# A copy of X opens Y's bank: fewer VectorE adds, and other orders, in a spectral layer with a gated feed-forward block

## The chip, the cores and the metric

The kernel runs on one core of one Trainium2 chip. A core has five engines, each with its own queue of instructions that it works off strictly in order: TensorE (PE; its weight loads are shown apart as PEld), VectorE (DVE), ScalarE (ACT), GpSimd (POOL) and SyncE (SP), which here only issues DMAs. They meet through semaphores. PE writes its products to PSUM, eight banks of 128 partitions by 512 fp32 numbers; DVE and ACT read and write PSUM, POOL works in SBUF alone here. The metric is the device time of one execution in microseconds (us), the median of several runs.

## What is computed

```python
# x: 2048 x 448; F1, F2: complex DFT matrices over sequence and features
def A(x):                       # FNet mixing: Real(DFT_seq(DFT_hidden(x)))
    a = x @ dft_hid_re.T
    b = x @ dft_hid_im.T
    return dft_seq_re @ a - dft_seq_im @ b
def B(x):                       # GEGLU
    return (gelu(x @ w_gate) * (x @ w_up)) @ w_down      # 448 -> 1792 -> 448
h  = x + A(layernorm(x))
out = h + B(layernorm(h))
```

Everything comes in and goes out as fp32.

## The kernel before

Every fp32 operand is split into two fp16 parts, a high one written by ACT (`hi_part`, L100) and the remainder, written by DVE (`lo_part`, L104 and L106). A product is then three products of parts, all summed in one PSUM bank. The matrix products that can be are done with seven products of half blocks instead of eight, after a scheme of Strassen's kind, so sums of blocks are formed ahead of the splits, and the results are put together from several banks.

There are four stages. **The feature DFT** (F) handles sixteen tiles of 128 rows of x. For each, `x_stats` takes mean and variance (DVE), `root` the square root (ACT), `rstd` the reciprocal with a correction step (DVE), `x_norm` the normalized row and its high part, `x_lo` the remainder. `x_turn_pe` transposes the first four tiles on PE and copies the result to SBUF with ACT (L371); the others are transposed by DMA (`x_turn`). `feature_mm` makes 22 products of 448 columns into two banks (L408), `feature_out` splits them into the operands `b` of the next stage; of three units (`S_UNITS`) it only copies them to fp32, POOL forms sums (`feature_sums`), and `feature_split` splits those.

**The sequence DFT** (U) has eight passes, each over eight units of the DFT matrices `wr`. `seq_sums` forms sums for a unit of S_UNITS (DVE), `seq_split` makes the fp16 parts `ws` (three buffers), `seq_mm` multiplies (L494): 24 products of 448 columns for a plain unit, 42 of 224 columns for an S unit, into four banks X, Y, Z, W. Two sets of four banks serve alternating passes. `seq_out` puts the four banks together with x, which `h_tile` has loaded, to two rows of h. Passes 0 to 3 are followed at once by the second layernorm's work (`ffn_moments`, `ffn_rstd`, `ffn_norm_act`, `ffn_sums`, `ffn_split`, `ffn_transpose`). The weights of gate and up are prepared in the same stretch (class `Weights`) and stored to `w_dram`.

The order in both DFT stages is set by a table. `slots` lists the F and U entries in PE's order; `plan(n, rank, what)` hangs other work on slot n, and the loop at the end records what hangs on a slot by rank and then the slot's products. Since engines work in order, that order is each engine's queue. The first three slots are written out by hand ahead of the loop.

**Gate/up** runs over 56 steps t (four quarters q of 512 rows, fourteen slices f of 128 hidden columns). A step makes seven products (class `GateUp`, L872): X takes A11·B11 and later A12·B21, Y takes S2·T2, then S3·T3, then A22·T4, and Z takes S1·T1 and S4·B22, six or five matmuls of 256 columns each and 39 in all. X alone (`u1`, L910, an ACT copy) is needed three times: `plus` (L882, DVE) adds it to Y as it stands after each of Y's three products. ACT makes the gelu of X (`g1`, L923) and of `c12` (L946); POOL makes the two multiplications (L939, L948). `gw_load(t + 2)` (L952, SP) loads the weights of step t + 2 into the buffer that step t - 1 used; there are three. In the first quarter ACT, DVE and POOL also prepare the down weights (`down_hi`, `down_lo`, `down_sums`).

**Down** is interleaved with steps 14 to 55 (L815, 21 products of 224 columns in each step), from sums that POOL and DVE form (`dn_sums`) and splits (`dn_split`); the last quarter is multiplied at the end (L1035).

## Time and profile before

| | |
|---|---|
| median of 3 runs | 738.9 us (736.61, 738.9, 739.53) |
| the profiled execution | 736.13 us, of which the span of its instructions is 734.3 us |
| PE busy | 712.6 us of the span, 5800 matmuls |
| DVE busy | 577.6 us |
| ACT busy | 322.0 us |
| POOL busy | 265.7 us |
| first product of a feature tile | 9.42 us from the start of the span |
| sequence DFT and its preparation | until 370.07 us |
| gate/up and down | 370.07 to about 698 us |

Times in the views are counted from the start of the span. "Idle before" a row is the time in which its engine stood still just ahead of it, with the instruction that ended the wait. A matmul's duration in the rows covers its way through the array; matmuls overlap, so one of 256 columns lasts 0.273 us but the next starts after about 0.11.

### The profile page before, as it was taken

To read this page: it belongs to the slowest core of one execution; us is meant where nothing else is said; L and a number is where in the kernel's file an instruction comes from. 1 tells how busy PE (TensorE), PEld (TensorE's weight loads), DVE (VectorE), ACT (ScalarE), POOL (GpSimd) and SP (SyncE) were. 2 spreads that over 40 slices of the span, in tenths; PEclk is the share of its full clock that TensorE was granted. 3 is DMA by queue.
4 is the path that set the end of the run, shared out by engine and by line. 5 is a ranking of instruction groups with operands and counts; after the bars stand their busy time and mean duration, and the time that the engine had idled before them with its cause. 6 is when DMAs were issued, how large, how long until landed. Compare 5 with 4: busy or idle time off the path is not lost.

```text
span 734.3 us, 14677 instructions
## 1 busy us (share of the span) xinstructions
PE 712.6 (97%) x5800; PEld 560.9 (76%) x5800; DVE 577.6 (79%) x1166; ACT 322.0 (44%) x624; POOL 265.7 (36%) x294
## 2 busy tenths in 40 slices
PE   7899999999999999999999989999999999999998
PEld 4455567676656566676778869999999999999998
DVE  5767849998989899999457788788787877989730
ACT  5556545445454545344234444345444334454310
POOL 4032140000000000020018886576676776858430
PEclk9999999999999999999999999999999999999999
DMA  8363345798878889686147745655648476565401
GB/s 320 91 156 80 79 149 172 255 234 259 240 266 241 271 238 304 235 319 200 69 167 266 277 170 177 189 182 173 180 147 232 172 217 224 181 222 202 151 14 63
DMA packets 72340, 142.90 MB, mean 195 GB/s; under 512 B 41296, under 2 KB 47568, under 8 KB 72272
## 3 DMA queue, kind: packets, MB, share of 16 engines
q1 hardware_dynamic: 72272, 141.97, 60.8%
q8 instruction: 45, 0.74, 0.4%
q14 instruction: 23, 0.19, 0.1%
HBM read 112.46 MB, written 20.19 MB: 181 GB/s over the span
## 4 chain that ended last, share of the span: by engine, by line
PE 65%; DVE 19%; ACT 7%; DMA 4%; issue 4%; POOL 2%; SPq 1%; ACTq 0%; DVEq 0%; POOLq 0%
PE acc L494 19%; PE pY L872 13%; PE acc_d L815 11%; PE pX L872 8%; PE pZ L872 8%; DVE ws L106 4%; DVE xs L104 2%; ACT ws L100 2%; DMA w_dram<-gu_w 2%; DVE gu_w L106 2%; ACT b L100 2%; DMA x<-in_x_dram 1%; PE last_Z L1035 1%; PE last_X L1035 1%; PE last_tr L1035 1%
## 5 line engine op out<-in xcount | busy, mean ns | idle before, releaser
L494 PE MATMUL acc<-b,ws 128*128 128x448 f16 (+1 forms) x1968 | 281.5, 305 | 4.5 <-DVE ws L106 4.4
L494 PEld LDWEIGHTS <-ws 128*128 128x128 f16 x1968 | 189.4, 98 | 96.0 <-DVE ws L106 9.6
L872 PEld LDWEIGHTS <-gw 128*128 128x128 f16 x2067 | 201.8, 98 | 25.9 <-issue 5.0
L872 PE MATMUL pY<-hops,gw 128*128 128x256 f16 x901 | 122.7, 273 | 4.2 <-DVE u L882 3.9
L815 PE MATMUL acc_d<-wd,dn_w 128*128 128x224 f16 x882 | 105.1, 259 | 0.0
L815 PEld LDWEIGHTS <-dn_w 128*128 128x128 f16 x882 | 85.1, 98 | 2.8
L198 POOL TENSOR_TENSOR wd_s<-wd 128x448 f32<-128x448 f32 x7 | 8.0, 1144 | 217.0 <-DMA wd<-in_w_down_dram 217.0
L106 DVE SCALAR_TENSOR_TENSOR ws<-wr,ws 128x1024 f16<-128x1024 f32 (+2 forms) x88 | 74.6, 871 | 14.8 <-ACT ws L100 14.2
L100 ACT ACTIVATE ws<-wr 128x1024 f16<-128x1024 f32 (+2 forms) x88 | 63.7, 756 | 49.3 <-issue 30.3
L872 PE MATMUL pX<-hops,gw 128*128 128x256 f16 x583 | 81.0, 273 | 0.0
L872 PE MATMUL pZ<-hops,gw 128*128 128x256 f16 x583 | 79.2, 273 | 0.0
L939 POOL TENSOR_TENSOR hh<-hh,g 128x256 f32<-128x256 f32 x42 | 36.8, 876 | 100.5 <-DVE hh L882 100.5
L882 DVE SCALAR_TENSOR_TENSOR u<-pY,u 128x256 f32<-128x256 f32 x112 | 47.0, 420 | 32.0 <-ACT c L946 15.9
L408 PEld LDWEIGHTS <-xT 128*128 128x128 f16 x352 | 34.6, 99 | 34.3 <-issue 3.9
L910 ACT ACTIVATE u<-pX 128x256 f32<-128x256 f32 x56 | 21.4, 382 | 86.3 <-PE pX L872 80.7
L104 DVE TENSOR_TENSOR dn_w<-dn_s,dn_w 128x640 f16<-128x640 f32 x42 | 52.7, 1255 | 1.6 <-ACT dn_w L100 1.4
L923 ACT ACTIVATE g<-pX 128x256 f32<-128x256 f32 x56 | 21.3, 380 | 70.5 <-PE pX L872 64.8
L408 PE MATMUL ab<-wh_hi,xT 128*128 128x448 f16 x224 | 46.5, 359 | 1.7 <-DVE b L106 1.7
L100 ACT ACTIVATE ws<-wsum 128x1024 f16<-128x1024 f32 x24 | 25.3, 1053 | 45.6 <-DVE wsum L468 45.6
L966 POOL TENSOR_TENSOR dn_s<-hh 128x256 f32<-128x256 f32 x42 | 43.9, 1046 | 0.0
L948 POOL TENSOR_TENSOR hh<-hh,c 128x256 f32<-128x256 f32 x42 | 37.3, 887 | 17.4 <-ACT c L946 17.4
L965 POOL TENSOR_TENSOR dn_s<-hh 128x256 f32<-128x256 f32 x42 | 42.4, 1010 | 0.0
(130 smaller groups left out, 932.3 us busy)
## 6 DMA issues: line engine op xcount, KB each, us to landing
gw<-w_dram SPq DMA_DIRECT2D x53, 896.0 KB, 4.7
wr<-in_w_seq_dram SPq DMA_DIRECT2D x64, 512.0 KB, 4.3
w_dram<-gu_w SPq DMA_DIRECT2D x14, 896.0 KB, 7.4
gu_raw<-in_w_gu_dram SPq DMA_DIRECT2D x28, 384.0 KB, 5.3
wd<-in_w_down_dram SPq DMA_DIRECT2D x14, 448.0 KB, 4.9
hx<-in_x_dram SPq DMA_DIRECT2D x8, 448.0 KB, 6.3
h_dram<-hx SPq DMA_DIRECT2D x8, 448.0 KB, 6.4
hr<-h_dram SPq DMA_DIRECT2D x8, 448.0 KB, 5.3
```

The source lines that it names most:

```text
L100: A.activation(dst, src, AF.Copy, scale=scale)
L104: V.tensor_sub(dst, src, hi)
L106: V.scalar_tensor_tensor(dst, src, scale, hi, op0=ALU.mult, op1=ALU.subtract)
L408: PE.matmul(feat[i][r][:, :D], xT[i][:, kx, :], w[:, kw, r * D : (r + 1) * D], start=n == 0, stop=n == 10,)
L494: PE.matmul(banks[k][:, cols], lhs, rhs, start=k not in begun, stop=stop, skip_group_check=True)
L815: PE.matmul(acc[k // 2][:, k % 2 * HD : (k % 2 + 1) * HD], a_of(la, a), b_of(lb, b), start=first and m == 0 and k % 2 == 0, stop=last and ...
L872: PE.matmul(ps, w[:, wl, wa + ws, :], ops[:, m + ms, :], start=first and n == 0, stop=last and n == len(terms) - 1, skip_group_check=True,)
L882: V.scalar_tensor_tensor(dst, ps, SC, other, op0=ALU.mult, op1=ALU.add)
L939: G.tensor_mul(c21, c21, self.g1)
L948: G.tensor_mul(c22, c22, self.c12)
L965: G.tensor_add(s[:, 0:2], t[:, 0:2], t[:, 2:4])
L966: G.tensor_sub(s[:, 2:4], t[:, 1:4:2], t[:, 0:4:2])
```

## The change

Nothing is left out of the computation, and the number of matmuls stays 5800. Five things change.

1. **Gate/up.** After the first product of X, ACT copies X's bank into Y's bank (`x_open`), and Y's three products are all added onto that copy (`y_open`, `y_mid`, `y_close`). Y then holds the sum that `plus` made, so `u2` and `u3` become ACT copies of Y, and the product with `g1` is taken straight from the bank by one DVE instruction; `plus` is left twice in a step instead of five times, and one of POOL's two multiplications goes. PE's order within a step is another: X of the next step is opened two or more products ahead of its Y, and in the first quarter Z between the two. For odd steps after the first quarter, Y's bank is the one that was `ps_tr`. `c12` has two buffers instead of one.
2. **Sequence DFT.** From pass 2 on, `seq_seed` has ACT copy x, times 64, into banks X and Y ahead of the pass's products, which are added onto it. `seq_out` then needs no sum with x: two DVE instructions of 448 columns go, and X and Y are read last instead of first. `h_tile` loads x five slots ahead of the pass. S units stand at places 2, 5 and 7 of a pass (1, 3 and 6 before).
3. **Square roots.** `root` is taken out of `x_stats` and `ffn_rstd` and planned by itself one slot later (`x_root`, `ffn_root`), in ACT's queue behind the copies of PE's results that the same slot asks for, with other work between it and `rstd` in DVE's queue.
4. **The beginning.** The order of the first tiles is rewritten: the first quarter of the feature weights is loaded ahead of the second tile of x, `wh_high(1)` goes to DVE and `wh_high(3)` to ACT, and the two halves of a PE transpose get a bank each instead of sharing one.
5. **Small moves.** The last `down_hi` and `down_lo` go behind the first quarter, `dn_sums(1)` two steps earlier, and the last four products use the banks in another order.

```diff
+    def ffn_root(q, j):
+        moments[q, j] = moments[q, j], root(moments[q, j], f"h{q}_{j}")
+
     def ffn_rstd(q, j):
-        tag = f"h{q}_{j}"
-        mv = moments[q, j]
-        moments[q, j] = mv, rstd(mv, root(mv, tag), tag, const)
+        mv, sd = moments[q, j]
+        moments[q, j] = mv, rstd(mv, sd, f"h{q}_{j}", const)
...
-        norm_x[tiles] = mv, root(mv, tag)
+        norm_x[tiles] = mv
+
+    def x_root(*tiles):
+        norm_x[tiles] = norm_x[tiles], root(norm_x[tiles], f"x{tiles[0]}")
...
     def x_turn_pe(i, k0, k1):
         if k0 == 0:
             xT_tile(i)
-            ptr[i] = ps_dft.tile([P, 8, P], F16, tag="A", name=f"xT_ps{i}")
+        t = ps_dft.tile([P, 8, P], F16, tag="A", name=f"xT_ps{i}_{k0}")
         for k in range(k0, k1):
-            PE.transpose(ptr[i][:, k, :], xs[i][:, k * P : (k + 1) * P], ident)
-        A.activation(xT[i][:, k0:k1, :], ptr[i][:, k0:k1, :], AF.Copy)
+            PE.transpose(t[:, k, :], xs[i][:, k * P : (k + 1) * P], ident)
+        A.activation(xT[i][:, k0:k1, :], t[:, k0:k1, :], AF.Copy)
...
+    def seq_seed(p):
+        banks, begun = seq_banks(p)
+        for g in range(2):
+            A.activation(banks[g][:, 0:D], hp[divmod(p, 2)][:, g], AF.Copy, scale=D_SC)
+            begun.add(g)
...
         A.activation(e[:, 1], Z[:, 0:HD], AF.Copy, scale=SC_Y)
-        stt(h[:, 0], X[:, 0:D], SC_Y, h[:, 0], op0=ALU.mult, op1=ALU.add)
+        if p < 2:
+            for g, ps in enumerate((X, Y)):
+                stt(h[:, g], ps[:, 0:D], SC_Y, h[:, g], op0=ALU.mult, op1=ALU.add)
...
-        for g in range(2):
-            V.tensor_add(h[:, g], h[:, g], e[:, 2 * g : 2 * g + 2].rearrange("p o d -> p (o d)"))
+        for g, ps in enumerate((X, Y)):
+            eg = e[:, 2 * g : 2 * g + 2].rearrange("p o d -> p (o d)")
+            if p < 2:
+                V.tensor_add(h[:, g], h[:, g], eg)
+            else:
+                stt(h[:, g], ps[:, 0:D], SC_Y, eg, op0=ALU.mult, op1=ALU.add)
...
-    for n, s in enumerate(S_UNITS):
-        mixed.insert(1 + n * 8 // len(S_UNITS), s)
+    for n, s in zip((2, 5, 7), S_UNITS):
+        mixed.insert(n, s)
...
                 plan(n - 7, 7, lambda i=i, j=i2: x_stats(i, j))
+                plan(n - 6, 2, lambda i=i, j=i2: x_root(i, j))
                 plan(n - 6, 5, lambda i=i, j=i2: x_rstd(i, j), lambda i=i, j=i2: x_bias(i, j))
...
-        plan(n + 1, 5, lambda q=q, j=j: ffn_stats(q, j, hp[q, j]))
+        for g in range(2):
+            plan(n + 1, 5, lambda q=q, j=j, g=g: ffn_moments(q, j, hp[q, j], g))
+        plan(n + 2, 2, lambda q=q, j=j: ffn_root(q, j))
+        plan(n + 2, 5, lambda q=q, j=j: ffn_rstd(q, j))
...
-    def open(self):
-        self.X, self.Y = self.bank(0), self.bank(1)
+    def x_open(self):
+        self.X = self.bank(0)
         self.mul(self.X, "A11", "B11", True)
-        self.mul(self.Y, "S2", "T2", True)
-        self.u1 = ftile("u1", 2, f"u1_{self.name}")
-        A.activation(self.u1, self.X, AF.Copy, scale=SC)
+        self.Y = self.bank(1)
+        A.activation(self.Y, self.X, AF.Copy)
+
+    def y_open(self):
+        self.mul(self.Y, "S2", "T2", False)
         self.u2 = ftile("u2", 2, f"u2_{self.name}")
-        plus(self.u2, self.Y, self.u1)
+        A.activation(self.u2, self.Y, AF.Copy, scale=SC)
...
+    def y_mid(self):
+        self.mul(self.Y, "S3", "T3", False)
         u3 = ftile("u3", 1, f"u3_{self.name}")
-        plus(u3, self.Y, self.u1)
+        A.activation(u3, self.Y, AF.Copy, scale=SC)
         plus(self.hidden(1), self.Z, u3)
...
+    def y_close(self):
         self.mul(self.Y, "A22", "T4", False)
+        V.scalar_tensor_tensor(self.hidden(0), self.Y, SC, self.g1, op0=ALU.mult, op1=ALU.mult)
...
-            dn_ahead(t)
-            cur.xy()
-            prev = cur
-            cur = GateUp(t + 1)
-            cur.open()
-            prev.yz()
+            cur.x_close()
+            nxt.x_open()
+            if prev:
+                prev.c_last()
+            cur.y_mid()
+            nxt.z_open()
+            nxt.y_open()
+            cur.y_close()
+            cur.z_close()
+            dn_ahead(t)
```

How the queues move is shown at three places. The first is ACT's queue in the feature DFT, where tile 10's and tile 11's products (`ab10`, `ab11`) are copied out of PSUM and the square root for the next pair of tiles (`sd_x6`) is taken. Before:

```order
L336 ACTIVATE x6_417<-x6_417,nb_x12_510,r_x12_504 128x448
L100 ACTIVATE xs6_545<-x6_417 128x448
L121 ACTIVATE sd_x6_594<-mv_x6_587,eps_t_79 128x2
L100 ACTIVATE b32_11_622<-ab11_0_598 128x448
L100 ACTIVATE b32_11_622<-ab11_1_599 128x448
L100 ACTIVATE b10_626<-b32_10_575 128x1568
L100 ACTIVATE b11_664<-b32_11_622 128x1568
```

And now:

```order
L340 ACTIVATE x6_421<-x6_421,nb_x12_514,r_x12_508 128x448
L100 ACTIVATE xs6_549<-x6_421 128x448
L100 ACTIVATE b32_11_624<-ab11_0_600 128x448
L100 ACTIVATE b32_11_624<-ab11_1_601 128x448
L121 ACTIVATE sd_x6_628<-mv_x6_591,eps_t_79 128x2
L100 ACTIVATE b10_630<-b32_10_579 128x1568
L100 ACTIVATE b11_668<-b32_11_624 128x1568
```

The square root, which needs DVE's statistics, has moved behind the two copies, which need PE's products alone.

The second is DVE's queue in pass 3 of the sequence DFT, around the layernorm of pass 2's rows (`mv_h1_0`, `r_h1_0`, `nb_h1_0`); `ws3_2` and `ws3_3` are the splits of the pass's units 2 and 3. Before:

```order
L175 BN_STATS st_h1_0_1_2217<-hx2_1885 128x6
L176 BN_AGGR mv_h1_0_2213<-st_h1_0_1_2217 128x2
L128 RECIPROCAL r_h1_0_2222<-sd_h1_0_2220 128x2
L129 TENSOR_SCALAR r_h1_0_2222<-mv_h1_0_2213 128x2
L130 TENSOR_TENSOR r_h1_0_2222<-r_h1_0_2222 128x2
L131 TENSOR_TENSOR r_h1_0_2222<-r_h1_0_2222 128x2
L132 SCALAR_TENSOR_TENSOR r_h1_0_2222<-r_h1_0_2222 128x2
L106 SCALAR_TENSOR_TENSOR gu_w8_2171<-gu_s8_2123,gu_w8_2171 128x512 x2
L106 SCALAR_TENSOR_TENSOR ws3_2_2280<-wr3_2_2069,ws3_2_2280 128x1024
L217 SCALAR_TENSOR_TENSOR nb_h1_0_2284<-mv_h1_0_2213,r_h1_0_2222 128x2
L106 SCALAR_TENSOR_TENSOR ws3_3_2317<-wr3_3_2128,ws3_3_2317 128x1024
```

And now:

```order
L175 BN_STATS st_h1_0_1_2217<-hx2_1520 128x6
L176 BN_AGGR mv_h1_0_2213<-st_h1_0_1_2217 128x2
L106 SCALAR_TENSOR_TENSOR gu_w8_2179<-gu_s8_2115,gu_w8_2179 128x512 x2
L106 SCALAR_TENSOR_TENSOR ws3_3_2256<-wr3_3_2079,ws3_3_2256 128x1024
L128 RECIPROCAL r_h1_0_2259<-sd_h1_0_2254 128x2
L129 TENSOR_SCALAR r_h1_0_2259<-mv_h1_0_2213 128x2
L130 TENSOR_TENSOR r_h1_0_2259<-r_h1_0_2259 128x2
L131 TENSOR_TENSOR r_h1_0_2259<-r_h1_0_2259 128x2
L132 SCALAR_TENSOR_TENSOR r_h1_0_2259<-r_h1_0_2259 128x2
L470 TENSOR_TENSOR wsum3_6_2265<-wr3_6_2120 128x512
L471 TENSOR_TENSOR wsum3_6_2265<-wsum3_6_2265,wr3_6_2120 128x256
L472 TENSOR_TENSOR wsum3_6_2265<-wsum3_6_2265,wr3_6_2120 128x256
```

Two splits now stand between the statistics and the reciprocal, and the sums of an S unit behind it.

The third is PE's queue in the first quarter of gate/up, from the last product of step 2, which ends the use of the buffer that step 5's weights (`gw5`) are loaded into, to step 5's first product. Each row stands for the first of five or six alike, which are left out. Before:

```order
L872 MATMUL pZ_2_4219<-hops0_156,gu_w2_3359 128x256
...
L872 MATMUL pZ_3_4285<-hops0_156,gw3_4155 128x256
...
L872 MATMUL pX_3_4246<-hops0_156,gw3_4155 128x256
...
L872 MATMUL pY_3_4247<-hops0_156,gw3_4155 128x256
...
L872 MATMUL pX_4_4312<-hops0_156,gw4_4217 128x256
...
L872 MATMUL pY_4_4313<-hops0_156,gw4_4217 128x256
...
L872 MATMUL pZ_4_4347<-hops0_156,gw4_4217 128x256
...
L872 MATMUL pX_5_4374<-hops0_156,gw5_4283 128x256
```

And now:

```order
L913 MATMUL pZ_2_4194<-hops0_156,gu_w2_3367 128x256
...
L913 MATMUL pX_3_4234<-hops0_156,gw3_4165 128x256
...
L913 MATMUL pX_4_4298<-hops0_156,gw4_4225 128x256
...
L913 MATMUL pY_3_4241<-hops0_156,gw3_4165 128x256
...
L913 MATMUL pZ_4_4318<-hops0_156,gw4_4225 128x256
...
L913 MATMUL pY_4_4305<-hops0_156,gw4_4225 128x256
...
L913 MATMUL pX_5_4358<-hops0_156,gw5_4289 128x256
```

Between the two ends there were 56 matmuls (Z 6, X 5, Y 6, X 6, Y 6, Y 5, Z 5, Z 6, X 5, Y 6), and there are 44 now (X 5, X 6, Y 6, Z 6, Y 6, Y 5, Z 5, X 5).

More of the change, by code (lines that the diff above doesn't have):

```diff
@@ L479, with seq_banks @@
     acc = {}
+    def seq_banks(p):
+        if p not in acc:
+            acc[p] = [ps_dft.tile([P, 512], F32, tag="AB"[p % 2], name=f"acc{p}_{k}") for k in range(4)], set()
+        return acc[p]
+    def seq_seed(p):
[3 more added lines that the diff above has]
+            begun.add(g)
     PRODUCTS = [(0, 0, 2, 0), (1, 2, 0, 1), (6, 1, 0, 0), (2, 6, 1, 1), (4, 3, 2, 1), (5, 5, 3, 0), (3, 4, 3, 1)]
@@ L486, in seq_mm @@
         if first:
-            acc[p] = [ps_dft.tile([P, 512], F32, tag="AB"[p % 2], name=f"acc{p}_{k}") for k in range(4)], set()
+            seq_banks(p)
         banks, begun = acc[p]
@@ L657 @@
         n = max(where["U", p, u] for u in range(N_UNIT)) + 1
-        plan(n - 6, 9, lambda p=p: h_tile(p))
+        if p < 2:
+            plan(n - 6, 9, lambda p=p: h_tile(p))
+        else:
+            n0 = min(where["U", p, u] for u in range(N_UNIT))
+            plan(n0 - 5, 9, lambda p=p: h_tile(p))
+            plan(n0 - 2, 4, lambda p=p: seq_seed(p))
         if p == N_PASS - 1:
@@ L675 @@
     x_load(0, (slice(0, 1),))
+    wh_load(0)
     x_load(0, (slice(1, 2),))
-    for k in range(4):
+    for k in range(1, 4):
         wh_load(k)
@@ L703 @@
     feature_mm(1, range(4))
-    wh_low(0)
+    wh_low(1)
     x_lo(2)
```

160 lines of the change are left out of this document (86 added, 74 removed).

## The prediction

> **What bounds the kernel now.** The first thing read is the engines' table of the page, then PE's waits.
>
> ```profile
> PE 712.6 (97%) x5800; PEld 560.9 (76%) x5800; DVE 577.6 (79%) x1166; ACT 322.0 (44%) x624; POOL 265.7 (36%) x294
> PE xT_ps L370 <- ACT xT L371: 5.8, 4, 2.3
> PE pY L872 <- DVE u L882: 4.5, 4, 2.3
> PE acc L494 <- DVE ws L106: 4.4, 10, 0.7
> PE ab L408 <- DVE b L106: 1.7, 4, 0.9
> PE xT_ps L370 <- ACT xs L100: 0.5, 1, 0.5
> PE pY L872 <- DVE hh L882: 0.3, 1, 0.3
> ```
>
> PE is the bound: it is busy for 97% of the span, and the matmuls stay 5800. The change can only give back what PE waits, or add waits. A recorded wait is a little too short, since it counts from the end of a matmul, not from where the next could have started:
>
> ```profile
> 387.45 1.36 PE L872 MATMUL pY<-hops,gw 128*128 128x256 f16 x11
> 388.66 1.36 PE L872 MATMUL pZ<-hops,gw 128*128 128x256 f16 x11
> ```
>
> Eleven matmuls take 388.66 - 387.45 = 1.21 us, 0.11 each, but eleven last 1.36 when the last one's way through the array counts: each wait costs 1.36 - 1.21 = 0.15 more than its row. The six rows, 17.2 us in 24 waits, are so worth 17.2 + 3.6 = 20.8 us. That is the ceiling of the gain, and each part below is a share of it.
>
> **The feature DFT: square roots behind the copies.** Here is ACT's timeline at the first disputed place, columns start, busy us, and in brackets the idle time before the row and its releaser.
>
> ```profile
> 45.95 0.58 ACT L100 ACTIVATE xs<-x 128x448 f16<-128x448 f32 x1
> 49.23 0.29 ACT L121 ACTIVATE sd_x<-mv_x,eps_t 128x2 f32<-128x2 f32 x1 [2.71 <-DVE mv_x L316]
> 49.44 0.96 ACT L100 ACTIVATE b<-ab 128x448 f32<-128x448 f32 x2
> 54.54 1.51 ACT L100 ACTIVATE b<-b 128x1568 f16<-128x1568 f32 x1 [2.75 <-POOL b L448]
> 57.22 0.96 ACT L100 ACTIVATE b<-ab 128x448 f16<-128x448 f32 x2
> ```
>
> ACT stands 2.71 us at a square root for DVE's statistics; the copies queued behind it (49.44) are for a bank that PE has finished. POOL's sums start that much later, ACT stands again 2.75 us for them (54.54), the copy at 57.22 is late, and PE waits for the split behind it (`ab <- DVE b`). With the root behind the copies they run at about 46.5 instead of 49.44. PE's four waits of 1.7 + 4 x 0.15 = 2.3 us are each under 0.9, less than the 2.71 that ACT wins. I take 2.2 us back, ends 0 (DVE turns out late by itself) and 2.3.
>
> **The beginning.** Four PE transposes' second halves wait for ACT's copy of the first half, 5.8 us, since both are in one bank. The longest is this:
>
> ```profile
> 22.22 0.69 DVE L104 TENSOR_TENSOR xs<-x,xs 128x64 f16<-128x64 f32 x2 [0.64 <-ACT xs L100]
> 23.40 0.39 PE L370 MATMUL xT_ps<-ident,xs 128*128 128x128 f16 x4
> 26.13 0.33 PE L370 MATMUL xT_ps<-ident,xs 128*128 128x128 f16 x3 [2.34 <-ACT xT L371]
> 32.72 0.54 PE L494 MATMUL acc<-b,ws 128*128 128x448 f16 x2
> ```
>
> Two banks take these waits away, but not all comes back, because DVE's queue becomes the limit: the fourth tile's remainder ends at 22.22 + 0.69 = 22.9, PE's transpose starts at 23.40. In the new queue DVE does what it did before it, with one 896-column conversion more (`wh_high(1)`), in a stretch in which it waited for that DMA, and without two small instructions' waits for ACT. I place the fourth transpose at 22.4. Behind it now stand 20 matmuls for tiles 0 to 2 and 22 for tile 3, at 0.19 us each (448 columns against 256, 0.11 x 448 / 256): 22.4 + 0.4 + 8.0 = 30.8, against 32.72 for the first product of the sequence DFT. Gain 1.9. Ends: 0.6 if DVE is 1.3 later, 4 if its queue runs free.
>
> **The sequence DFT.** PE's and DVE's timelines of one pass:
>
> ```profile
> 220.03 3.81 PE L494 MATMUL acc<-b,ws 128*128 128x224 f16 x36 [0.68 <-DVE ws L106]
> 224.18 21.84 PE L494 MATMUL acc<-b,ws 128*128 128x448 f16 x156 [0.34 <-DVE ws L106]
> 246.38 9.85 PE L494 MATMUL acc<-b,ws 128*128 128x448 f16 x54 [0.35 <-DVE ws L106]
> 256.90 3.81 PE L494 MATMUL acc<-b,ws 128*128 128x224 f16 x36 [0.68 <-DVE ws L106]
> 206.25 0.17 DVE L128 RECIPROCAL r_h<-sd_h 128x2 f32<-128x2 f32 x1 [0.36 <-ACT sd_h L121]
> 209.37 0.15 DVE L217 SCALAR_TENSOR_TENSOR nb_h<-mv_h,r_h 128x2 f32<-128x2 f32 x1
> 211.95 1.23 DVE L106 SCALAR_TENSOR_TENSOR ws<-wr,ws 128x1024 f16<-128x1024 f32 x1 [2.42 <-ACT ws L100]
> 218.00:255.00 37.00, 35.60 (x249) 23.59 (x247) 33.51 (x70) 18.23 (x31) 0.00 (x0) 1.00 0.83 252
> L528 DVE TENSOR_TENSOR hx<-hx,e 128x448 f32<-128x448 f32 x16 | 9.2, 618 | 0.0
> L219 ACT ACTIVATE xn_h<-hx,nb_h,r_h 128x448 f32<-128x448 f32 x16 | 11.3, 753 | 10.4 <-DVE nb_h L217 10.3
> hx<-in_x_dram SPq DMA_DIRECT2D x8, 448.0 KB, 6.3
> ```
>
> The pattern repeats after 256.90 - 220.03 = 36.87 us, with three waits in it worth 1.37 + 0.45 = 1.8: PE alone needs 35.1. DVE works 33.51 of 37 us (third number of the window's row) and stands 2.42 of them at one place: after `nb_h` it needs ACT's half of a split, which is behind ACT's two `xn_h` (0.75 each), which need `nb_h`. Its own work fits in 35.1, its work with that stand does not. So the waits are DVE's load plus a loop between DVE and ACT.
>
> What the change does to it: two of DVE's four additions per pass go from pass 2 on, 2 x 0.62 = 1.2 us (the two that read X and Y then add `e` in their place). The wait for the root, 0.36, goes behind two splits. The loop over `nb_h` stays, but DVE now has the S unit's sums to do ahead of it, and I count 1.9 us of stand where 2.42 was. DVE so needs 33.5 - 1.2 + 1.9 = 34.2 in passes 2 and 3, under 35.1; in passes 0 and 1, where `seq_out` keeps its additions, 35.4, a little over. ACT gets two seeds per pass. No row shows ACT writing to PSUM; its nearest rows of 448 columns last about 0.5 to 0.6 (`b` at 49.44, `xs` at 45.95), it is busy 18.23 of 37, and the bank to be seeded has been read a whole pass before: 1.1 us beside other work. Were it three times that, ACT would still stand idle a third of the pass. The seeds also stand ahead of a split in ACT's queue and wait for the load of x; that is issued three slots (13 us) ahead and lasts 6.3 in the last row above, of the page's DMA issues. Of 4.4 + 10 x 0.15 = 5.9 us I expect 4.7 back. Ends 0 and 5.9.
>
> **Gate/up, what goes.** Three rows from the timelines of PE and ACT:
>
> ```profile
> 428.10 0.71 PE L872 MATMUL pY<-hops,gw 128*128 128x256 f16 x5 [1.38 <-DVE u L882]
> 439.48 0.70 PE L872 MATMUL pY<-hops,gw 128*128 128x256 f16 x5 [2.29 <-DVE u L882]
> 437.50 0.74 ACT L100 ACTIVATE dn_w<-dn_s 128x640 f16<-128x640 f32 x1 [1.27 <-POOL dn_s L966]
> L939 POOL TENSOR_TENSOR hh<-hh,g 128x256 f32<-128x256 f32 x42 | 36.8, 876 | 100.5 <-DVE hh L882 100.5
> L910 ACT ACTIVATE u<-pX 128x256 f32<-128x256 f32 x56 | 21.4, 382 | 86.3 <-PE pX L872 80.7
> ```
>
> Both long waits come from POOL's backlog: ACT stands for POOL's sums, DVE for ACT, and `u` comes late. The multiplication that leaves POOL is 0.88 a step; `plus` leaves DVE three times, and the new readers of Y are on ACT. ACT gets 2 copies of 0.38 more in each step, 0.8 us, and was busy 44%. The five rows of pY are worth 4.8 + 5 x 0.15 = 5.6.
>
> The new wait is X to Y: `y_open` needs ACT's copy of a product that has just ended. Between them lie 12 matmuls in the first quarter (1.3 us) and 13 behind it, and the copy takes 0.38: 0.9 is left for ACT to be late. At the very first step ACT loads the gelu table between, and I count 0.5 there, and 0.5 for down weights in the queue: 5.6 - 1.0 = 4.6. Ends 2 and 5.6.
>
> **Gate/up, what comes.** A load of weights in the first quarter, with PE around it, and the loads' times over that quarter:
>
> ```profile
> 384.40 0.71 PE L872 MATMUL pZ<-hops,gu_w 128*128 128x256 f16 x5
> 385.14 4.58 SPq L952 DMA_DIRECT2D gw<-w_dram  x2
> 391.06 0.38 PE L872 MATMUL pX<-hops,gw 128*128 128x256 f16 x2
> 425.24 1.31 PEld L872 LDWEIGHTS <-gw 128*128 128x128 f16 x13 [0.24 <-DMA gw<-w_dram]
> DMA to landing us min/median/max: 4.4/4.7/6.0
> ```
>
> SP issues at 385.14, as soon as the last product on the old weights ends (384.40 + 0.71). The new ones are used at 391.06, 5.92 us later, after 56 matmuls. The longest of the 14 loads, 6.0, is the one that PE waits for at 425.24: there is no slack left. The change leaves 44 matmuls, 4.8 us, less the 0.2 until SP issues: 4.6. A load of the median 4.7 is then 0.1 late and the longest 1.4. A wait also lengthens the time that the next load has, so of two neighbours only the later counts in full. Going through the loads in their order, with 4.6 taken off each and the neighbour's wait off the rest, I get 3.7 us for the quarter. Ends: 0.7 if all are median, and 6.5 x 1.4 = 9 if every second is as long as the longest. SP's own queue has nothing new ahead of these loads. Behind the first quarter a step is 39 x 0.11 + 21 products of 224 columns (0.11 x 224 / 256 each) = 6.3 us, half as long again as in the first, so nothing is due there.
>
> [...]
>
> **The sum.** Against the profiled execution (736.1; its span of 734.3 and 1.8 around it): 2.2 + 1.9 + 4.7 + 4.6 - 3.7 = 9.7, which gives 726.4. It lies 2.8 us under the median of the runs and 0.5 under the lowest, so I add 0.6: **727 us**.
>
> **The rivals.** *The loads come in time* (they start 1.3 us earlier after each step, perhaps with less traffic beside them): 727 - 3.7 = 723. [...] For it speaks the smallest of 4.4, against it the wait that exists already at 425.24.
>
> *DVE stays the bound of the sequence DFT.* With 35.4 of 35.1 us in two passes, any further stand of DVE brings PE's waits back: 727 + 4.7 = 732. For it: 33.51 of 37 us busy and `nb_h`'s loop intact. Against it: 1.2 us less work.
>
> *Wait for wait*: this, and loads near the upper end together, 727 + 4.7 + 4 = 736, no change that can be told. A change that doesn't do what it says (copies that run late at every place) ends here too.
>
> *ACT behind POOL* ends slower. In the later quarters Y's copy, `u2` and `u3` stand in ACT's queue behind `dn_w`, which at 437.50 waited 1.27 for POOL. Now three releases of PE hang on that queue, where two hung on DVE. An event costs PE 2.29 + 0.15 = 2.44 us, in a kernel that otherwise stands at 727: from seven of them in the 42 steps of the later quarters on it passes 742.6 (0.5% over the median), and one in every fifth step, eight in all, gives 727 + 8 x 2.44 = 747. For it: the two rows above are exactly that. Against it: POOL loses 0.88 us of work in each step.
>
> **How the numbers follow.** Forecast 0.48, loads in time 0.17, DVE stays the bound 0.20, wait for wait 0.09, ACT behind POOL 0.06. About 0.5% (3.7 us) is what a measurement of this kernel can tell from no change. Below 735.2 lie the first three: 0.85; within 0.5% are 0.09, above 742.6 are 0.06. The likeliest case's own range is 722 to 731 (start 0.6 to 4, loads 0.7 to 6). For 8 in 10 it goes from 719 (loads in time and the upper end at the beginning) to 733.
>
> **What would show it.** Right: no `xT_ps <- ACT xT` and no `ab <- DVE b` among PE's waits; the first `acc` near 30.8; passes of the sequence DFT 35 us apart; in the first quarter of gate/up waits for `DMA gw`, together near 3.7 us, and none after it. Wrong: `acc <- DVE ws` with ten waits as before, waits of pY or pX for ACT in every step, or a first quarter of 60 us without waits for loads.

## The result: 729.9 us, 1.1% less

| | before | changed |
|---|---|---|
| median, runs of the same call | 737.75 us (736.44 to 739.53) | 729.86 us (726.95 to 731.49) |
| ratio | | 0.9887, 95% interval 0.9844 to 0.9931 |
| the profiled execution | 736.13 us, span 734.3 | 728.71 us, span 726.9 |

The forecast was 727 (719 to 733). From profile to profile the gain is 7.4 us, where the sum had 9.7.

The page's row for PE and all of PE's waits in the changed kernel (total us, times, longest):

```profile
PE 712.0 (98%) x5800; PEld 561.6 (77%) x5800; DVE 510.6 (70%) x1043; ACT 365.0 (50%) x748; POOL 207.9 (29%) x237
PE pX L913 <- DMA gw<-w_dram: 4.5, 3, 1.6
PE xT_ps L374 <- DVE xs L104: 2.3, 3, 1.9
PE acc L508 <- DVE ws L106: 1.5, 3, 0.7
PE pw L94 <- POOL eps_t L86: 1.4, 1, 1.4
PE xT_ps L374 <- ACT xs L100: 1.1, 1, 1.1
PE pZ L913 <- DVE hh L923: 0.3, 1, 0.3
PE ab L412 <- DVE wh_lo L106: 0.3, 1, 0.3
```

The waits `xT_ps <- ACT xT`, `ab <- DVE b` and `pY <- DVE u` of before are gone, `acc <- DVE ws` has fallen from ten waits to three, and a new one stands first: three times 1.3 to 1.6 us for weights of gate/up.

Where the time went is read best from PE's timeline, at the first product of each stage. Before:

```profile
106.69 0.54 PE L494 MATMUL acc<-b,ws 128*128 128x448 f16 x2
370.07 0.82 PE L872 MATMUL pX<-hops,gu_w 128*128 128x256 f16 x6
434.11 0.64 PE L815 MATMUL acc_d<-wd,dn_w 128*128 128x224 f16 x5
```

And changed:

```profile
31.82 1.11 PE L508 MATMUL acc<-b,ws 128*128 128x448 f16 x5
103.65 1.05 PE L508 MATMUL acc<-b,ws 128*128 128x448 f16 x4
362.53 0.82 PE L913 MATMUL pX<-hops,gu_w 128*128 128x256 f16 x6
429.95 0.93 PE L855 MATMUL acc_d<-wd,dn_w 128*128 128x224 f16 x8
```

The first `acc` (32.72 before) ends the beginning, the second row shown, the first one behind the last feature tile, ends the feature DFT, `pX` the sequence DFT, and `acc_d`, the first product of down, the first quarter of gate/up. The differences of these starts, for this profile and for those of all experiments below (us):

| kernel | beginning | feature DFT | sequence DFT | first quarter | the rest |
|---|---|---|---|---|---|
| before | 32.72 | 73.97 | 263.38 | 64.03 | 300.2 |
| changed | 31.82 | 71.82 | 258.88 | 67.42 | 297.0 |
| gu_before | 32.19 | 71.83 | 259.33 | 65.35 | 301.7 |
| gu_only | 34.74 | 73.94 | 263.44 | 66.03 | 297.7 |
| gw_four | 31.43 | 71.83 | 258.90 | 62.46 | 297.0 |
| no_wd | 31.61 | 71.82 | 258.78 | 64.06 | 297.0 |
| no_seed | 31.86 | 71.83 | 260.19 | 67.32 | 297.0 |
| s_places | 32.16 | 71.82 | 260.13 | 67.34 | 297.0 |
| roots_back | 32.80 | 75.73 | 260.51 | 70.09 | 297.0 |
| norm_late | 30.53 | 71.86 | 256.95 | 65.86 | 296.9 |
| warm | 30.96 | 71.85 | 259.57 | 66.91 | 297.0 |
| wl3_dve | 28.57 | 72.86 | 258.76 | 66.52 | 296.9 |
| best | 28.31 | 72.86 | 259.14 | 62.46 | 297.0 |
| best_norm | 28.08 | 72.85 | 256.87 | 62.47 | 297.0 |

Edits of 1 us hardly show in the times of whole runs, so they are read from this table. How well a stage repeats where no edit touches it, it tells too: the feature DFT within 0.1 us, the sequence DFT from 258.8 to 259.6 over the changed kernel and six others, the rest within 0.1 (gu_only's 297.7 is told of below); the beginning and the first quarter vary by 1 us and more, in good part for reasons that the last section names. The two rows on top hold the result: 0.9 us come from the beginning, 2.15 from the feature DFT, 4.5 from the sequence DFT. The 0.9 is the least certain of them: the beginning of before comes to 34.74 in gu_only, where no edit touches it, and the changed one to 30.53 in norm_late. In gate/up the first quarter lost 3.4 and the rest won 3.3, nothing in all.

### The profile page after: what moved, and what is told of

Read it like the earlier page. It is cut to its first block, busy times and chain, and to the rows that moved or that the text cites. A ratio compares the mean times of both kernels' runs of the same rounds, so it can differ in the third digit from the quotient of the medians.

```text
span 726.9 us, 14535 instructions
## 1 busy us (share of the span) xinstructions
PE 712.0 (98%) x5800; PEld 561.6 (77%) x5800; DVE 510.6 (70%) x1043; ACT 365.0 (50%) x748; POOL 207.9 (29%) x237
## 4 chain that ended last, share of the span: by engine, by line
PE 79%; DVE 10%; DMA 5%; ACT 3%; issue 1%; SPq 0%; DVEq 0%; ACTq 0%
PE acc L508 28%; PE pY L913 13%; PE acc_d L855 11%; PE pZ L913 8%; PE pX L913 8%; PE ab L412 7%; DMA gw<-w_dram 3%; DVE ws L106 2%; DVE xs L104 1%; DMA wr<-in_w_seq_dram 1%; PE last_Z L1079 1%; PE last_X L1079 1%; PE last_Y L1079 1%; DMA gu_raw<-in_w_gu_dram 1%; DVE gu_w L106 1%
## 5 line engine op out<-in xcount | busy, mean ns | idle before, releaser
L913 PE MATMUL pZ<-hops,gw 128*128 128x256 f16 x583 | 80.9, 273 | 0.4 <-DVE hh L923 0.3
L992 POOL TENSOR_TENSOR hh<-hh,c 128x256 f32<-128x256 f32 x42 | 31.3, 746 | 145.2 <-ACT c L990 145.2
L104 DVE TENSOR_TENSOR dn_w<-hh,dn_w 128x256 f16<-128x256 f32 x42 | 19.6, 466 | 53.1 <-ACT dn_w L100 53.1
L1010 POOL TENSOR_TENSOR dn_s<-hh 128x256 f32<-128x256 f32 x42 | 52.8, 1256 | 0.0
L104 DVE TENSOR_TENSOR dn_w<-dn_s,dn_w 128x640 f16<-128x640 f32 x42 | 46.2, 1101 | 6.3 <-ACT dn_w L100 5.2
L957 ACT ACTIVATE u<-pY 128x256 f32<-128x256 f32 x56 | 21.4, 382 | 57.3 <-PE pY L913 57.3
L952 ACT ACTIVATE pY<-pX 128x256 f32<-128x256 f32 x56 | 20.6, 368 | 51.9 <-PE pX L913 51.7
L1009 POOL TENSOR_TENSOR dn_s<-hh 128x256 f32<-128x256 f32 x42 | 37.9, 902 | 0.0
L971 ACT ACTIVATE u<-pY 128x256 f32<-128x256 f32 x56 | 21.4, 382 | 27.2 <-PE pY L913 26.9
L100 ACT ACTIVATE ws<-wsum 128x1024 f16<-128x1024 f32 x24 | 25.2, 1051 | 18.9 <-DVE wsum L472 18.9
```

The lines of the kernel that those rows point to most:

```text
L100: A.activation(dst, src, AF.Copy, scale=scale)
L104: V.tensor_sub(dst, src, hi)
L913: PE.matmul(ps, w[:, wl, wa + ws, :], ops[:, m + ms, :], start=first and n == 0, stop=last and n == len(terms) - 1, skip_group_check=True,)
L957: A.activation(self.u2, self.Y, AF.Copy, scale=SC)
L992: G.tensor_mul(c22, c22, self.c12)
L1009: G.tensor_add(s[:, 0:2], t[:, 0:2], t[:, 2:4])
```

## The experiments

**Which half of the change pays: gu_before and gu_only.** Two kernels put the parts together crosswise: the changed DFTs with the old gate/up, and the old DFTs with the new gate/up (from the pools of gate/up on, the file is the other kernel's).

```
 gu_before: after.py up to     fpool = ctx.enter_context(tc.tile_pool(name="fpool" ...
            before.py from there on, and
-    at(side, (25, 4), lambda: ffn_rstd(NB - 1, 1))
+    at(side, (25, 4), lambda: (ffn_root(NB - 1, 1), ffn_rstd(NB - 1, 1)))
 gu_only:   the same with before.py and after.py exchanged
```

> The changed kernel with gate/up and down as they were before; both DFT stages and the beginning stay changed. My reading (gate/up gave back about 4.9 us of waits and took 5.0 for late loads): gate/up and down last 364.2 us as before, the waits of PE for loads in the first quarter go, the waits for DVE's u come back (about 4.5 us), and the time is that of the changed kernel, 728 to 730. Rival (the copy of X into Y carries the gain, the DFT stages less than their spans say): 733 or more.

> The kernel before with the new gate/up alone; beginning and both DFT stages as before. My reading (what the copy of X gives back, the loads take): the first quarter lasts 67.4 instead of 64.0, what follows 261.6 instead of 264.8, and the time is that of the kernel before within 1 us. Rival (the copy pays by itself): 734 or less. Rival (it costs by itself): 741 or more.

gu_before took 730.16 us, ratio to before 0.9892 (0.9865 to 0.992), the same as the whole change; gu_only 737.86 against 738.04, ratio 1.0003 (0.9986 to 1.002). So the whole measured gain is that of the beginning and the DFTs, and the copy of X into Y with its new order is worth nothing as it stands, to within 1.5 us by gu_only's interval. That was the reading, and the waits for `u` came back in gu_before (4.1 us in four), but some details differ. From the list of PE's waits in gu_before:

```profile
PE pX L912 <- DMA gw<-w_dram: 1.6, 2, 1.2
```

The old order too can wait for loads, 1.6 us here and hardly at all in the profile of before, with the same window of 56 matmuls. And gate/up of gu_before lasted 367 instead of 364 us; the stretch of half clock shown in the last section is 1.7 us of that. In gu_only the first quarter lasts 66.0 and not the expected 67.4, since its loads cost PE 3.0 us where the changed kernel's cost 4.5, and a wait that the changed kernel does not have (`pZ <- DVE c`, 0.9 us) makes the rest 297.7. Its beginning, the same as before's, is 2.0 us longer: a remainder `xs` on DVE met POOL's work (2.37 us at 16.36, against 0.68 in before), and the clock fell twice and not once (its mean is 0.995, against 0.998 in before).

**The late loads: gw_four and no_wd.** In the changed kernel the first quarter's loads stand like this: PE's timeline at a late one, SP's queue at that time (`wd` are the down weights), and the time from issue to landing of all 14, then of the one issued at 377.70 and of the one at 387.73.

```profile
383.81 0.83 PE L913 MATMUL pX<-hops,gw 128*128 128x256 f16 x6 [1.34 <-DMA gw<-w_dram]
...
374.47 0.33 SPq L190 DMA_DIRECT2D wd<-in_w_down_dram  x1
377.70 4.58 SPq L996 DMA_DIRECT2D gw<-w_dram  x2
383.64 0.33 SPq L190 DMA_DIRECT2D wd<-in_w_down_dram  x1
387.73 4.58 SPq L996 DMA_DIRECT2D gw<-w_dram  x2
...
DMA to landing us min/median/max: 4.4/4.6/6.3
DMA to landing us min/median/max: 6.1/6.1/6.1
DMA to landing us min/median/max: 4.4/4.4/4.4
```

The load of gate/up weights that is issued 3.2 us behind one of down weights lands after 6.1 us and is late; the one issued 4.1 behind lands after 4.4 and is not. The other two late loads are issued 2.6 behind and land after 6.3, and the fifth that follows one of down weights, 4.4 behind, after 4.5. The first experiment gives the loads a step more, with a fourth buffer in the room that hh's second buffer leaves empty in the first quarter; the second leaves out five loads of down weights, so that part of its result is made from other weights.

```
 gw_four
+        if t == 0:
+            gw_load(3)
...
-        if 0 < t < N_GU - 2:
-            gw_load(t + 2)
+        if 0 < t < N_GU - 2 and t != 12:
+            gw_load(t + 3 if t < 12 else t + 2)
...
     def gw_load(t):
-        gw[t] = w_tile(f"gw{t}", ring if t % 3 < 2 else ring3)
+        k = t % 4 if t < 12 else t % 3
+        if k == 3:
+            room = fpool.tile([P, NC, 4, TQ], F32, tag="hh", bufs=2, name="gw_room") if t == 3 else None
+            more.extend([room] if room is not None else [])
+            gw[t] = more[0].rearrange("p n k t -> p (n k t)").bitcast(F16)[:, : 28 * P]
+        else:
+            gw[t] = w_tile(f"gw{t}", ring if k < 2 else ring3)
 no_wd
                 if n + 2 < NC:
-                    down_load(n + 2)
+                    wd32[n + 2] = wd32[n]
```

> The changed kernel with a fourth weight buffer in the first quarter of gate/up, in the room of hh's second buffer, and each load issued a step earlier. My reading (each late load is one that overlaps a load of down weights, and only its distance to its use is at fault): the three waits, 4.5 us in the rows and 5.0 from matmul to matmul, go; gate/up and down last 359.4 instead of 364.4, and the time is about 725. Rival (the first quarter is bound by the bytes of its loads): waits for loads of 3 us or more stay. Rival (a wait of PE for ACT or DVE takes their place): the loads' waits go, the stage stays above 362.

> The changed kernel without the five loads of down weights in the first quarter of gate/up; weights already there are taken in their place, so that part of the result is left out. My reading (a load of 896 KB is late only where a load of down weights runs beside it): all loads of that quarter land after 4.4 to 4.7 us, PE waits less than 0.5 us for them in all instead of 4.5, and the first quarter lasts 62.5 to 63 instead of 67.4. Rival (the loads are too slow by themselves for a window of 4.6): waits of 1 us or more stay.

gw_four: 725.0 us, ratio to before 0.9824 (0.9802 to 0.9846); the waits for loads are gone from PE's list, the first quarter lasts 62.46, and gate/up 359.4, as expected. The loads did not become faster, they became slower, and nothing waits for them:

```profile
DMA to landing us min/median/max: 4.5/6.4/7.2
```

no_wd: 13 of the 14 loads landed in time, with only one wait, and the first quarter lasted 64.06. So the loads of down weights are behind 3.4 of the 5.0 us that gw_four wins. But that one wait contradicts "only where"; its load, issued at 403.10, landed after 5.8 us. PE's row:

```profile
408.94 0.83 PE L913 MATMUL pX<-hops,gw 128*128 128x256 f16 x6 [1.07 <-DMA gw<-w_dram]
```

No other large transfer was issued beside it; what held it up was not settled. With 5.8 us for that load, the window of 4.6 us was too short even without those of down weights.

**The sequence DFT: no_seed, s_places, roots_back, norm_late.** Three edits undo one part each, the fourth tries the cause that is left.

```
 no_seed
-            plan(n0 - 2, 4, lambda p=p: seq_seed(p))
     (and seq_out as before)
 s_places
-    for n, s in zip((2, 5, 7), S_UNITS):
+    for n, s in zip((1, 3, 6), S_UNITS):
 roots_back
-                plan(n - 6, 2, lambda i=i, j=i2: x_root(i, j))
+                plan(n - 7, 7, lambda i=i, j=i2: x_root(i, j))
...
-        plan(n + 2, 2, lambda q=q, j=j: ffn_root(q, j))
-        plan(n + 2, 5, lambda q=q, j=j: ffn_rstd(q, j))
+        plan(n + 1, 5, lambda q=q, j=j: ffn_root(q, j))
+        plan(n + 1, 5, lambda q=q, j=j: ffn_rstd(q, j))
 norm_late
-            plan(n + 2, 6, lambda q=q, j=j: ffn_norm_act(q, j, hp[q, j]))
+            plan(n + 3, 4, lambda q=q, j=j: ffn_norm_act(q, j, hp[q, j]))
```

> The changed kernel without the copies of x into X's and Y's banks; every pass adds x on DVE as before. My reading (DVE is still the bound in passes 1 to 3): two DVE instructions of 0.62 more in passes 3 to 7; pass 3 lasts 36.4 to 37 instead of 35.9, pass 4 up to 35.6 instead of 34.8, passes 5 to 7, which have no layernorm work, stay at 34.8; in all 1 to 2.4 us more. Rival (the gain came from the places of the S units or the roots alone): all passes within 0.2 us of the changed kernel's.

> The changed kernel with the S units at places 1, 3 and 6 of a pass, as before. My reading: DVE's work is the same, but without an S unit's sums between the reciprocal and nb it stands longer at the loop with ACT (2.4 us instead of 1.8), so passes 1 to 3 last about 0.5 longer each: the sequence DFT 260.4 instead of 258.9. Rival (only the amount of work counts): 258.9 within 0.3. Rival (the places carry the whole gain): passes of 36.9 as before.

> The changed kernel with the square roots back beside their statistics, in both DFT stages; everything else stays. My reading: in the feature DFT the four waits for the splits of ab come back, 2.2 us between the first product of the sequence DFT and the last of the feature DFT; in the sequence DFT DVE stands 0.36 more for the root in passes 1 to 4, which costs 0.3 us in each of passes 1 to 3. Rival (the root's place does not matter, other orders removed the waits): both stages within 0.3 us of the changed kernel's.

> The changed kernel with nb and ACT's two xn of the second layernorm planned one slot later, behind the next unit's split. My reading (the waits left in the sequence DFT come from DVE's stand of 1.8 us for ACT's half of a split, which is queued behind xn): that stand goes, passes 1 to 3 last 34.8 instead of 35.4, 35.3 and 35.9, the sequence DFT 257.0 instead of 258.9. Rival (DVE then stands for xn itself at the sums that read it): passes as in the changed kernel, or longer.

The passes, each 246 products long, counted back on PE's timeline from the first `pX` (us; in the expectations I numbered them one too low, so their "passes 1 to 3" are passes 2 to 4 here):

| kernel | pass 1 | 2 | 3 | 4 | 5 to 7 each |
|---|---|---|---|---|---|
| changed | 34.77 | 35.37 | 35.31 | 35.87 | 34.77 |
| no_seed | 34.77 | 35.12 | 36.23 | 36.42 | 34.77 |
| s_places | 34.77 | 36.49 | 35.58 | 35.57 | 34.77 |
| roots_back | 34.77 | 36.11 | 35.67 | 35.98 | 34.77 |
| norm_late | 34.77 | 34.77 | 34.77 | 34.77 | 34.77 |

Against the 258.8 to 259.6 of the kernels with this stage unedited, each part is worth 0.6 to 1.7 us, and none carries the gain alone: without the copies of x the stage is 1.3 us longer than the changed kernel's, in the two passes that then have DVE's additions back beside the layernorm; with the old places of the S units 1.25, nearly all of it in pass 2 and not 0.5 in each as I had it; with the old roots 1.6. Each of these is one profile. In the seven kernels with the stage unedited pass 2 lasts 35.4 in all and pass 3 from 35.2 to 35.5, but pass 4 anything from 35.4 to 36.3, so differences in pass 4 alone tell little. In passes 5 to 7, which have no layernorm work, none of the four edits costs PE anything. The times of no_seed, s_places and roots_back, of one run each, are 730.04, 730.2 and 737.9 us. In the feature DFT the roots cost 3.9 us in this order (75.73 against 71.82), more than the 2.2 of before, with six waits `ab <- DVE b` of up to 1.1 instead of four.

norm_late went to the loop between DVE and ACT. In the changed kernel DVE's rows, and ACT's beside them, still show it in pass 4:

```profile
239.31 0.15 DVE L214 SCALAR_TENSOR_TENSOR nb_h<-mv_h,r_h 128x2 f32<-128x2 f32 x1
241.25 1.21 DVE L106 SCALAR_TENSOR_TENSOR ws<-wr,ws 128x256 f16<-128x256 f32 x2 [1.78 <-ACT ws L100]
...
239.50 1.41 ACT L216 ACTIVATE xn_h<-hx,nb_h,r_h 128x448 f32<-128x448 f32 x2 [3.55 <-DVE nb_h L214]
240.81 0.92 ACT L100 ACTIVATE ws<-wr 128x256 f16<-128x256 f32 x2
```

DVE stands 1.78 us for a split's high part, which ACT does behind its two `xn_h`, which need `nb_h`. With both one slot later, in norm_late, DVE goes on at once behind `nb_h`, and PE is busy for the whole of the window (second number of the last row):

```profile
237.15 0.15 DVE L214 SCALAR_TENSOR_TENSOR nb_h<-mv_h,r_h 128x2 f32<-128x2 f32 x1
237.22 0.55 DVE L565 TENSOR_TENSOR gu_s<-gu_raw 128x384 f32<-128x384 f32 x1
...
218.00:253.00 35.00, 35.00 (x251) 24.04 (x249) 32.41 (x68) 19.22 (x32) 0.00 (x0) 1.00 0.89 273
```

DVE works 32.4 us of 35, no less than in the changed kernel (32.36 in its pass 4), and all seven passes last 34.77. It still stands 1.75 us for ACT's half of a split within this pass, at 252.33, and PE waits for none of that. So with the additions gone it was not the amount of DVE's work that bound these passes, but where it stood still. In the beginning and the first quarter this kernel differs from the changed one without an edit there, hence its 723.9 us.

**The beginning: wl3_dve and warm.** In the changed kernel PE waits 1.12 and 1.86 us at the third tile. The rows of PE, DVE and POOL:

```profile
15.02 0.34 PE L374 MATMUL xT_ps<-ident,xs 128*128 128x128 f16 x3 [1.12 <-ACT xs L100]
17.23 0.27 PE L374 MATMUL xT_ps<-ident,xs 128*128 128x128 f16 x1 [1.86 <-DVE xs L104]
...
10.71 1.08 DVE L106 SCALAR_TENSOR_TENSOR wh_lo<-wh_raw,wh_hi 128x896 f16<-128x896 f32 x1
14.28 2.75 DVE L106 SCALAR_TENSOR_TENSOR wh_lo<-wh_raw,wh_hi 128x896 f16<-128x896 f32 x1
...
14.19 1.89 POOL L400 TENSOR_TENSOR wh_lo<-wh_raw,wh_hi 64x896 f16<-64x896 f32 x1
```

The same DVE instruction takes 1.08 us at 10.71 and 2.75 at 14.28, when POOL has begun one of its own 0.09 us earlier. And behind it the granted clock (third number from the right) is at half for 3.4 us, while PE works on the products:

```profile
17.00:18.00 1.00, 0.58 (x5) 0.41 (x6) 1.00 (x4) 0.47 (x1) 0.00 (x0) 0.64 0.78 296
18.00:19.00 1.00, 1.00 (x5) 0.45 (x4) 0.97 (x3) 0.80 (x3) 0.00 (x0) 0.50 0.13 49
...
20.00:21.00 1.00, 1.00 (x5) 0.40 (x4) 0.53 (x2) 0.40 (x1) 0.00 (x0) 0.66 0.00 0
```

One experiment moves POOL's work on this part to DVE, a little later; the other keeps PE busy in its wait with transposes that nobody reads.

```
 wl3_dve
-    wh_low(3, G)
     x_stats(2)
...
+    wh_low(3)
     feature_mm(0, range(8, 11))
 warm
         for k in range(k0, k1):
+            for _ in range({0: 18, 3: 28}.get(k, 0) if i == 2 else 0):
+                PE.transpose(t[:, 7, :], ident, ident)
             PE.transpose(t[:, k, :], xs[i][:, k * P : (k + 1) * P], ident)
```

> The changed kernel with the remainder of the feature weights' fourth part made by DVE, behind the fourth tile's remainder, instead of by POOL at 11 to 16 us. My reading (DVE's remainder of the third part takes 2.75 us instead of 1.09 because POOL works beside it): it takes 1.1; PE's wait for xs of 1.9 falls below 0.4; the fourth tile's transposes come at 21 to 22 instead of 23.5, the first product of the sequence DFT at 29 to 30.5 instead of 31.8. Rival (DVE is slow there for the loads, which move 388 GB/s): it still takes over 2.5 us, and the extra DVE work makes the start later.

> The changed kernel with 46 idle transposes of the identity on PE, 18 ahead of the third tile's transposes and 28 ahead of the one among them that waits for DVE, all into an unused part of the same bank. My reading (the clock falls to half because PE stands still there): the granted clock stays at 1.0 in the first 40 us of the profile; PE still waits for DVE's remainder, the first product of the sequence DFT comes about 1.5 us earlier (31.8 to about 30.3), and nothing else changes. Rival (the clock falls at that time for another reason, or any pause is enough): 3.4 us of clock 0.5 between 15 and 25 us as before, and 31.8.

In wl3_dve the instruction takes 1.08, in warm the clock is 1.00 over the whole stretch:

```profile
14.16 1.08 DVE L106 SCALAR_TENSOR_TENSOR wh_lo<-wh_raw,wh_hi 128x896 f16<-128x896 f32 x1
...
15.00:25.00 10.00, 9.34 (x84) 5.94 (x82) 8.35 (x19) 4.37 (x10) 1.68 (x1) 1.00 0.34 126
```

The first reading holds: with POOL's work gone the same DVE instruction takes its plain 1.08, while the loads move 378 GB/s beside it as in the changed kernel (384), so POOL and not the loads had stretched it. wl3_dve brings the first `acc` to 28.57, 3.25 earlier and a little better than expected; 1.04 of it is given back in the feature DFT, where two waits `ab <- DVE b` (0.8 us) come up, which I had not reckoned with.

The second reading, that the clock falls because PE stands still and that the transposes keep it up, is likely but not shown by this one profile. norm_late has the beginning unedited, with the same two waits of 1.12 and 1.86 us, and its clock did not fall either. The fourth tile's transposes in the changed kernel, and in norm_late:

```profile
23.49 0.55 PE L374 MATMUL xT_ps<-ident,xs 128*128 128x128 f16 x7
22.19 0.55 PE L374 MATMUL xT_ps<-ident,xs 128*128 128x128 f16 x7
```

From the third tile's first transpose to the fourth's there are 8.47 us in the changed kernel, 7.01 in norm_late and 7.02 in warm. So the fall costs 1.5 us here, and of wl3_dve's 3.25 some 2.0 are left against norm_late's first `acc` at 30.53. For the transposes speak the runs: three of warm's four had a mean clock of 1.0, against two of the 17 runs of the eight kernels that have this beginning without them. warm brings the first `acc` to 30.96, not 30.3; its first product came 0.29 later by chance, and the 18 transposes put the third tile back by 0.3 more, so against the changed kernel's profile the edit is worth 1.15 and not 1.5. Its time is 727.9 (0.9868, 0.9842 to 0.9893), which does not stand clear of the changed kernel's.

**What beats both: best and best_norm.** best is gw_four with wl3_dve; best_norm has norm_late as well. The diffs are those above.

> The changed kernel with the fourth weight buffer in the first quarter and with the remainder of the feature weights' fourth part on DVE. My reading (both gains stand in different stages and add): the first product of the sequence DFT at 28.6, the sequence DFT's end at about 360, gate/up and down 359.4, span 719.6, time 721.5 to 723. Rival (the earlier end of one stage only makes another wait): 725 or more.

> The kernel of the run before with nb and xn one slot later as well. My reading: 1.9 us less in passes 1 to 3, span 717.7, time 719.5 to 721. Rival (DVE then stands for xn): no gain over the run before, or a loss.

best took 722.34 us (0.9791, 0.9768 to 0.9814), best_norm 719.09 (0.9742, 0.9721 to 0.9762): the gains of three stages add. Of best_norm's 717.2 us PE is busy 99%:

```profile
PE 709.3 (99%) x5800; PEld 561.8 (78%) x5800; DVE 509.8 (71%) x1044; ACT 364.9 (51%) x748; POOL 202.2 (28%) x235
```

## Why the prediction was right, point by point

| term | forecast | measured |
|---|---|---|
| feature DFT | 2.2 | 2.15 |
| beginning | 1.9 | 0.9 |
| sequence DFT | 4.7 | 4.5 |
| gate/up, what goes | 4.6 | 4.8 |
| gate/up, what comes | -3.7 | -4.9 |
| sum | 9.7 | 7.4 |

The measured gate/up splits so: the three late loads cost 5.0 us from matmul to matmul against 0.12 in the profile of before, and the two stages together changed by 0.1.

*The likeliest case was the one that came.* No rival took its place: the loads did not come in time, DVE kept three waits of ten, and ACT is not held up by POOL in the later quarters, where PE waits for no copy of Y at all.

*The beginning* came out 1.0 us short at one step: "I place the fourth transpose at 22.4". It came at 23.49; from there to the first `acc` it took 8.33 us, where 8.4 were set. The new queue of DVE was taken as running undisturbed; in fact one instruction of it ran against POOL's and cost 1.7 us (2.75 - 1.08). Without this meeting the transpose comes at 20.24 (wl3_dve), with it but without the fall of the clock at 22.19 (norm_late). So that 22.4 was so near was luck: a meeting that the working did not have made up for a queue that runs freer than reckoned, and the fall of the clock then took the 1 us. The meeting was there to be seen in the trace of before, in which the same pair of instructions meets. That profile has one fall of the clock too, at 8.46 to 11.87, so the measured 0.9 is the difference of two beginnings that both had one.

*The late loads* were right in mechanism and place, and the term was too small by 1.2 us. I took the loads' times in the order in which the trace of before has them. Most of them, though, land after 4.4 to 4.8 us, and those of 6.1 to 6.3 are those that meet a load of down weights; which ones these are is set by the new order. The profile of before could not give their length: there, loads issued 3.2 to 3.8 us behind one of down weights land after 4.45 to 6.0. In hindsight the working would have been: three loads of 6.2 against 4.6, 1.6 each, or 4.8, and with 0.15 for each refill 5.2 us.

*The sequence DFT* came out right in its sum, with a wrong step inside. DVE's need of 34.2 us in the two seeded passes, "under 35.1", was to leave no wait there; its work and its stand were met (32.4 us of work in pass 4, and 1.78 of stand where I had 1.9), but PE still waited, most of all in pass 4. A sum over a pass does not say whether a split is ready when it is due. PE alone needs 34.77, not 35.1 (passes 6 and 7 of before last that long), which gave the gain back again.

*ACT's new work* cost what the nearest rows said. The copies, in the page's groups and in ACT's timeline:

```profile
L952 ACT ACTIVATE pY<-pX 128x256 f32<-128x256 f32 x56 | 20.6, 368 | 51.9 <-PE pX L913 51.7
254.85 0.99 ACT L493 ACTIVATE acc<-hx 128x448 f32<-128x448 f32 x2
```

That is 0.368 us against the 0.38 taken for the copy into a bank of 256 columns, and 0.5 for 448 columns. PE waited for such a copy once, 0.08 us at the very start of gate/up, where I had set 0.5 aside.

## What to carry to other kernels

An edit that moves the first use of a loaded buffer forward has to be charged the whole window from the last use to the next first one; here 1.3 us less window took back all that the new accumulation had won, and a fourth buffer, in room that was empty in just that stage, gave it back. When an engine's load fits into the span but another engine still waits for it, look for the loop in its queue, not for less work: moving three instructions by one slot was worth more than removing two additions a pass. And a wait of PE can cost more than its row shows: behind those of 2.22 us in roots_back and 2.28 us in gu_before the clock was at half for 3.4 us, 1.7 us of work beside the wait.

## What the runs showed of the hardware

**Behind some waits of about 2 us PE's clock was at half, behind others at 1.00.** In roots_back PE waits 2.22 us for a load in the first quarter, and then:

```profile
391.25 1.27 PE L913 MATMUL pX<-hops,gw 128*128 128x256 f16 x6 [2.22 <-DMA gw<-w_dram]
...
391.00:392.00 1.00, 0.75 (x5) 0.61 (x6) 0.00 (x0) 0.00 (x0) 0.00 (x0) 0.74 1.07 409
392.00:393.00 1.00, 1.00 (x7) 0.69 (x6) 0.00 (x0) 0.45 (x2) 0.00 (x0) 0.50 0.86 251
393.00:394.00 1.00, 1.00 (x6) 0.71 (x5) 0.00 (x0) 0.35 (x2) 0.68 (x1) 0.50 0.68 276
394.00:395.00 1.00, 1.00 (x8) 0.72 (x6) 0.42 (x1) 0.28 (x1) 0.04 (x1) 0.55 0.14 55
```

At half speed for (1 - 0.74) x 2 + 1 + 1 + (1 - 0.55) x 2 = 3.4 us, which costs 1.7 us of work beside the wait itself. gu_before shows the same behind a wait of 2.28, and the profile of before has a wait of 2.29 for the same `u` at the same place, with the clock at 1.00 behind it (the first two rows are gu_before's, the last is of before, whose wait ends at 439.48):

```profile
434.07 1.22 PE L912 MATMUL pY<-hops,gw 128*128 128x256 f16 x5 [2.28 <-DVE u L922]
434.00:435.00 1.00, 0.93 (x5) 0.66 (x5) 0.97 (x3) 0.00 (x0) 1.00 (x3) 0.54 0.00 0
...
440.00:441.00 1.00, 1.00 (x12) 0.92 (x11) 1.00 (x2) 0.00 (x0) 1.00 (x2) 1.00 0.00 0
```

gu_before's stretch at half is 3.4 us long too: (1 - 0.54) x 2 + 1 + 1 + (1 - 0.75) x 2, with 0.50 in 435 to 437 and 0.75 in 437 to 438. What decides between the two outcomes is not shown; the waits, 2.28 and 2.29 us for the same `u`, are alike. The two waits of 1.12 and 1.86 us at the third tile had both outcomes as well: of the eight profiles with that beginning unedited seven have a fall that starts between 16.0 and 18.9, and one, norm_late, has none. Much of the spread of the times goes with it: the changed kernel's four runs had mean clocks of 1.0, 0.998, 0.997 and 0.995 and took 726.95, 728.71, 731.49 and 731.0 us, while best_norm, which has no wait over 1.4 us left in its profile, ran four times at 1.0 within 719.05 to 719.84. In warm, three of four runs were at 1.0, and one of six of best fell to 0.995 (725.54 us).

**Beside one of POOL's instructions a DVE instruction of 1.08 us took 2.75.** The DVE instruction that began 0.09 us behind POOL's (14.28 against 14.19) ended 0.95 us behind POOL's end (17.03 against 16.08), about its own length of 1.08: this looks as if it did not run slower but began its work when POOL was done, which the rows do not show directly. The trace of before has the same, and one meeting without it:

```profile
15.00 1.08 DVE L106 SCALAR_TENSOR_TENSOR wh_lo<-wh_raw,wh_hi 128x896 f16<-128x896 f32 x1
17.35 2.02 DVE L106 SCALAR_TENSOR_TENSOR wh_lo<-wh_raw,wh_hi 128x896 f16<-128x896 f32 x1
...
13.90 2.45 POOL L395 TENSOR_SCALAR wh_raw<-wh_raw 64x896 f32<-64x896 f32 x1
16.43 1.99 POOL L396 TENSOR_TENSOR wh_lo<-wh_raw,wh_hi 64x896 f16<-64x896 f32 x1
```

Against POOL's two-input instruction DVE again ends 0.95 us behind POOL's end (19.37 against 18.42); against the one-input instruction that runs from 13.90 to 16.35 it takes its plain 1.08, and so it does in gu_only (15.36, inside 13.76 to 16.22). So this instruction was late beside POOL's TENSOR_TENSOR (2.75 and 2.02 us) and not beside its TENSOR_SCALAR (1.08), as far as POOL's rough spans can tell.

**The loads issued a step earlier took longer to land.** The median of the first quarter's loads rose from 4.6 to 6.4 us in gw_four, and the stage became 5 us shorter: the same 896 KB took from 4.4 to 6.3 us in the changed kernel and from 4.5 to 7.2 here, where PE waited for none of them.
